# The first 14 steps of two fused layers, issued from one written-out sequence of operations

## The chip, the cores and the metric

The kernel runs on one core of one Trainium2 chip. Its engines are TensorE (PE in the profile; its weight loads are PEld), VectorE (DVE), ScalarE (ACT), GpSimd (POOL) and SyncE (SP), which here only issues DMAs. Each engine executes its own queue of instructions strictly in the order in which the program put them there, and waits on semaphores for the other engines. The metric is the device time of one execution in microseconds, as the median of several executions.

## The reference

```python
def sm(a, b):                      # softmax over the last axis
    s = scale * (a @ b.transpose(0, 2, 1))
    e = np.exp(s - s.max(-1, keepdims=True))
    return e / (e.sum(-1, keepdims=True) + 1e-09)
agent_v = sm(agents, k) @ v        # 49 agents over 12480 tokens of 128 features
x = sm(q, agents) @ agent_v        # 12480 x 128

h = x @ w_in                       # layer 1, 128 -> 2048
g = np.where(h >= 1, h, np.where(h <= -1, 0.0, (h + 1) ** 2 / 4))
x = g @ w_out                      # 2048 -> 128
h = x @ w_in2                      # layer 2, 128 -> 2048
g = s * np.maximum(h, 0) ** 2 + b
out = g @ w_out2
```

## The kernel before

The 12480 tokens are cut into 25 blocks: the first of 256, 23 of 512, the last of 448. A prologue (some 66 us) loads keys, values and weights, splits each weight into a high and a low part, and folds the agents' values into the first layer's weights (`awh`, `awl`). Then comes a loop of *steps*. A step `n` of a layer is two of the 16 slices of 128 hidden features of one block, so a block has 8 steps; steps 0 to 7 are the block of 256 tokens (tiles of 128x512 elements), the later ones blocks of 512 (128x1024).

The operations of a step, with the lines of the profile. Layer 1: `H(1, n)` (L567, PE, the products into a PSUM tile `h`), `relu` (L583, ACT, reads `h`, writes `x`), `square` (L589, ACT, `x` in place), `cap` (L593, DVE, reads `h` and `x`, writes `x`), `hi` (the high part `gh`, on ACT at L602 or on DVE at L604), `lo` (the low part `gl`, DVE, L609), `O(1, n)` (L649, PE, six matmuls into `y` from `gh` and `gl`). Layer 2 has `H(2, m)`, `relu` (L585), `square`, `hi`, `lo` and `O(2, m)` into `o`, without a cap. When a block's eight `O(1)` are done, `evac(1, ...)` copies `y` to `yh` (ACT, L668) and `yl` (DVE, L671), the input of layer 2. The caption of a tile tells the layer only with its buffer numbers; `x_14` is step 14.

For each block there is a softmax over the agents as well: `q_scores` (PE, L153, tile `qs`), a copy (ACT, L160, `qe`), maximum, difference (DVE), exponential (ACT, L174), sum, 1e-9, reciprocal, product (DVE), and the high and low halves of `ptok` (DVE, L182, L183); then `q_transpose` (PE, L196, `tp`) and a copy to `pt` (ACT, L201), which `H(1)` reads.

What sets the order: the program runs under a manual schedule, so each engine's queue has the order in which Python calls the operations. In the loop, step `n` puts on PE, in this order, `H(1, n)`, the scores of a softmax if one is due, a transpose if due, `O(1, n-2)`, `H(2, m)`, `O(2, m-2)` with `m = n - 11` (string `POR`); and on ACT and DVE the order of `ORD`, or of `ORDR` in the first 11 steps. The DVE and ACT operations of a softmax wait in the list `fillers` and are issued one at a time, one by each `lo` and one by each letter F; `q_transpose` first issues all that are left (L192). `sums_column` (three DVE operations on `csum` and `bcol`) goes through the same list, from step 11 on.

PSUM: all of `h`, `qs` and `tp` share one ring of 3 tiles of two banks; `y` and `o` have one bank each. `x`, `gh` and `gl` have 4 buffers each in SBUF.

`PAT1` tells for steps 0 to 10 of layer 1 whether `hi` runs on ACT (1) or DVE (0), and it is DVE after that.

Of the kernel before, what the change touches and what calls it, by code (L numbers as in the profile page):

```python
# [18 lines left out]
def kernel(  # L19
# [24 lines left out]

    GR, XB, UB, WB, KV = 4, 4, 4, 2, 7
    WARM, CD = 10, 1
    PAT1, PAT2, TL = "01010101010", "11011101", 11

# [16 lines left out]
        "A0 k0 k1 A1 k2 k3 k4 B0 k5 k6 k7 k8 B1 k9 k10 k11 k12 C0 q0 v0 v1 v2 C1 v3 v4 v5 v6 D0 v7 v8 v9 v10 v11 "  # L67
        "v12 D1 q1"
    )
    WORD = "A0 A1 B0 B1 C0 C1 D0 D1".split()  # L70
    POR = "H1 QS QT O1 H2 O2".split()
    NR, ORDR, ORD = 11, (
        "T2 R1 Y y R2 Q G2 C2 S1 M1 c1 G1 L1 L2 Z F"
    ).split(), (
        "R1 T2 S1 Q Y G2 R2 C2 L1 F M1 y L2 F Z G1 c1"
    ).split()
    QS, QT, DX = (7, 6, 3), (6, 5, 1), 1
    MASK_H = 0x7FFFFE00
    WBIAS = -8.0 * 896 * 2 ** 20
    TB = 512  # L80
# [65 lines left out]
    def q_scores(t):  # L146
        if t >= NB:
            return []
        qt = q_t.pop(t)
        sc = ps_h(f"qs{t}")  # L150
        scv = sc[:, 0, 0:4 * NA].rearrange("p (c a) -> p c a", a=NA)
        for i, c0 in enumerate(subs(t)):
            nc.tensor.matmul(out=scv[:, i, :], lhsT=qt[:, c0:c0 + P], rhs=aT, start=True, stop=True)  # L153
        e = small.tile([P, 4, NA], F32, tag="qe", name=f"qe{t}")
        mx = small.tile([P, 4], F32, tag="qm", name=f"qm{t}")
        sm = small.tile([P, 4], F32, tag="qsm", name=f"qsm{t}")
        pt = ptok[t % NPT]
        parts = [(P, 0, len(subs(t)))]
        ops = [
            lambda n=n, a=a, b=b: nc.scalar.activation(out=e[:n, a:b, :], in_=scv[:n, a:b, :], func=ACTF.Copy)  # L160
            for n, a, b in parts
        ]
        qev.extend(ops)
        ops = []
        for n, a, b in parts:
            ev, mv, sv = e[:n, a:b, :], mx[:n, a:b], sm[:n, a:b]
            wide = [n, b - a, NA]
            ph, pl = pt[:n, a:b, 0:NA], pt[:n, a:b, LO:LO + NA]
            ops += [
                lambda ev=ev, mv=mv: nc.vector.tensor_reduce(out=mv, in_=ev, op=ALU.max, axis=AX.X),  # L170
                lambda ev=ev, mv=mv, wide=wide: nc.vector.tensor_tensor(
                    out=ev, in0=ev, in1=mv.unsqueeze(2).to_broadcast(wide), op=ALU.subtract
                ),
                lambda ev=ev: nc.scalar.activation(out=ev, in_=ev, func=ACTF.Exp, scale=scale),  # L174
                lambda: None,
                lambda ev=ev, sv=sv: nc.vector.tensor_reduce(out=sv, in_=ev, op=ALU.add, axis=AX.X),
                lambda sv=sv: nc.vector.tensor_scalar_add(sv, sv, 1e-9),
                lambda sv=sv: nc.vector.reciprocal(out=sv, in_=sv),
                lambda ev=ev, sv=sv, wide=wide: nc.vector.tensor_tensor(
                    out=ev, in0=ev, in1=sv.unsqueeze(2).to_broadcast(wide), op=ALU.mult  # L180
                ),
                lambda ev=ev, ph=ph: nc.vector.tensor_copy(out=ph, in_=ev),  # L182
                lambda ev=ev, ph=ph, pl=pl: nc.vector.tensor_tensor(  # L183
                    out=pl, in0=ev, in1=ph.bitcast(F32), op=ALU.subtract
                ),
            ]
        return ops

    def q_transpose(t):
        if t >= NB:  # L190
            return
        fill(len(fillers))  # L192
        w = blocks[t][1]
        tp = ps_h(f"tp{t}")[:, 0, :]
        for i, c0 in enumerate(subs(t)):
            nc.tensor.matmul(  # L196
                out=tp[:, c0:c0 + P], lhsT=ptok[t % NPT][:, i, :], rhs=ident_r,
                start=True, stop=True,
            )
        pt_t[t] = ptp.tile([P, TB], F32R, tag="pt", name=f"pt{t}")  # L200
        qev.append(lambda: nc.scalar.activation(out=pt_t[t][:, :w], in_=tp[:, :w], func=ACTF.Copy))  # L201
# [333 lines left out]
    def sums_column():  # L535

        c = csum.rearrange("p (k d) -> p k d", d=P)
        return [
            lambda: nc.vector.tensor_tensor(
                out=c, in0=c, in1=ident.unsqueeze(1).to_broadcast([P, TB // P, P]), op=ALU.mult  # L540
            ),
            lambda: nc.vector.tensor_reduce(out=bcol, in_=csum, op=ALU.add, axis=AX.X),
            lambda: nc.vector.tensor_scalar_mul(bcol, bcol, b_sb[:, 0:1]),
        ]
# [9 lines left out]
    def H(layer, n):  # L554
        t, j = divmod(n, JP)
        w = blocks[t][1]
        h = ps_h(f"h{layer}_{n}")
        for i in range(2):
            sl = slice((2 * j + i) * P, (2 * j + i + 1) * P)
            if layer == 1:  # L560
                rhs = pt_t[t][:, :w]
                ops = [(awh, rhs), (awl, rhs)]
            else:
                yh, yl = y_hl[t]
                ops = [(wi2h, yh[:, :w]), (wi2h, yl[:, :w]), (wi2l, yh[:, :w])]
            for m, (a, r) in enumerate(ops):
                nc.tensor.matmul(  # L567
                    out=h[:, i, :w], lhsT=a[:, sl], rhs=r, start=(m == 0), stop=(m == len(ops) - 1)
                )
        hp[layer, n] = h  # L570
# [8 lines left out]
    def relu(layer, n):  # L579
        gx[layer, n] = ring("x", layer, n, F32, XB)  # L580
        x, h = gv(gx, layer, n), gv(hp, layer, n)
        if layer == 1:
            nc.scalar.activation(out=x, in_=h, func=ACTF.Relu, scale=0.5, bias=0.5)  # L583
        else:
            nc.scalar.activation(out=x, in_=h, func=ACTF.Relu)  # L585

    def square(layer, n):
        x = gv(gx, layer, n)
        nc.scalar.activation(out=x, in_=x, func=ACTF.Square)  # L589
# [5 lines left out]
    def hi(layer, n, on_act):  # L595
        kind = GH(layer, n)
        if (kind == "1") != on_act:
            return
        gh[layer, n] = ring("gh", layer, n, F32R, GR)
        x, a = gv(gx, layer, n), gv(gh, layer, n)  # L600
        if on_act:
            nc.scalar.activation(out=a, in_=x, func=ACTF.Copy)  # L602
        else:
            nc.vector.tensor_copy(out=a, in_=x)  # L604
# [12 lines left out]
    def GH(layer, n):  # L617
        if layer == 1:
            return PAT1[n] if n < len(PAT1) else "0"
        return PAT2[n % len(PAT2)] if n < NS - TL else "0"  # L620
# [37 lines left out]
    def evac(layer, part):  # L658
# [14 lines left out]
        else:  # L673
# [5 lines left out]
            nc.sync.dma_start(out=outT[:, t0:t0 + w], in_=osb[:, :w])  # L679
            del done[2]  # L680

    with tc.manual_schedule():
        prologue()
        late = ctx.enter_context(tc.tile_pool(name="late", bufs=1))
        for n in range(NS + D + D2):
            t, j = divmod(n, JP)
            m = n - D
            a1, a2, b2 = n < NS, 0 <= m < NS, 0 <= m - 1 < NS
            b1 = 0 <= n - 1 < NS
            if j == 0:  # L690
                load_q(t + 2)
            for c in POR:
                if c == "H1" and a1: H(1, n)
                if c == "H2" and a2: H(2, m)
                if c == "O1" and 0 <= n - D1 < NS: O(1, n - D1)
                if c == "O2" and 0 <= m - D2 < NS: O(2, m - D2)
                if c == "QS" and n == 0: fillers.extend(q_scores(1))
                if c == "QS" and j == QS[min(t, 2)]: fillers.extend(q_scores(t + 2))
                if c == "QT" and j == QT[min(t, 2)]: q_transpose(t + 1)
            if n == NR:  # L700
                fillers.extend(sums_column())
            if m == NS:
                last_step(False)
            b2 = 0 <= m - 1 < NS - 1
            a2 = 0 <= m < NS - 1
            for c in (ORDR if n < NR else ORD):
                if c == "T2" and b2: square(2, m - 1)
                if c == "Q": q_evac()
                if c == "Y": evac(1, "h")
                if c == "y": evac(1, "l")  # L710
                if c == "Z": evac(2, "")
                if c == "G2" and b2: hi(2, m - 1, True)
                if c == "G1" and a1: hi(1, n, True)
                if c == "R1" and a1: relu(1, n)
                if c == "S1" and a1: square(1, n)
                if c == "R2" and a2: relu(2, m)
                if c == "M1" and a1: cap(n)
                if c == "c1" and a1: hi(1, n, False)
                if c == "C2" and b2: hi(2, m - 1, False)
                if c == "L1" and b1: lo(1, n - 1)  # L720
                if c == "L2" and b2: lo(2, m - 1)
                if c == "F": fill()
            if m == NS - 1:
                last_step(True)
# [35 lines left out]
```

## Time and profile before

| | us |
|---|---|
| median of 3 executions (1128.07 to 1128.37) | 1128.16 |
| the profiled execution | 1129.3 |
| its span, first to last instruction | 1126.6 |
| PE busy | 1093.7 |
| DVE busy | 986.5 |
| ACT busy | 971.8 |

The profile is of one execution. Its times count from the first instruction of the span. Busy times of an engine count overlapping instructions once; a matmul's end is modelled. "Granted clock" is the clock that TensorE was given, as a share of 2.4 GHz: 1.00, or 0.50 for 1.2 GHz. In the span's stretch up to about 66 us stands the prologue; step 0 of layer 1 begins at 66.28 us, step 14 at 114.05 us.

### The profile page before, as it was taken

The page shows a single profiled execution, that of the slowest core. Times are in us where ns is not written, and L with a number is a line of the kernel's source. Part 1 is how long each engine was busy: PE and PEld are TensorE (multiplying, and loading weights), DVE is VectorE, ACT ScalarE, POOL GpSimd, SP SyncE. Part 2 cuts the span into 40 slices and gives each one's busy share as a digit, 9 for nine tenths or more (in the row PEclk, how much of TensorE's full clock was granted, in tenths as well). Part 3 has the DMA queues.
Part 4 walks back from the last instruction along what each step waited for, and adds up shares of the span by engine and source line. Part 5 has one row for each costly group of instructions (what it writes and reads, how often), then busy time and mean ns, then how long its engine had stood idle before and what let it go on. Part 6 is the DMA issues. An engine that isn't in the chain of part 4 may idle for free.

```text
span 1126.6 us, 13210 instructions
## 1 busy us (share of the span) xinstructions
PE 1093.7 (97%) x5044; PEld 883.1 (78%) x5044; DVE 986.5 (88%) x1191; ACT 971.8 (86%) x1128; POOL 0.9 (0%) x7
## 2 busy tenths in 40 slices
PE   7877999999999999999999999999999999999998
PEld 3665888888888888888888888888888888888887
DVE  7867998898898898898898898898898898898886
ACT  6966899889889889889889888888888888889886
POOL 0000000000000000000000000000000000000000
PEclk9988999999999999999999999999999999999999
DMA  9910000000000000000000000000000000000000
GB/s 354 394 40 10 1 15 19 1 19 19 1 19 19 1 19 19 1 19 19 1 19 19 1 19 19 1 20 19 1 19 20 1 19 18 1 10 10 1 10 17
DMA packets 16254, 34.81 MB, mean 31 GB/s; under 512 B 1792, under 2 KB 6720, under 8 KB 15680
## 3 DMA queue, kind: packets, MB, share of 16 engines
q1 hardware_dynamic: 16192, 33.98, 8.5%
q8 instruction: 39, 0.64, 0.2%
q14 instruction: 23, 0.19, 0.1%
HBM read 27.58 MB, written 6.39 MB: 30 GB/s over the span
## 4 chain that ended last, share of the span: by engine, by line
PE 91%; DVE 5%; ACT 2%; DMA 1%; issue 0%; SPq 0%; DVEq 0%
PE h L567 39%; PE o L649 24%; PE y L649 24%; PE qs L153 2%; DVE x L593 1%; DMA k<-in_kT 1%; PE tp L196 1%; DVE gl L609 1%; PE av L422 1%; ACT x L589 1%; DVE mxs L379 1%; ACT x L583 1%; PE st L405 0%; DVE wt L264 0%; DVE gh L604 0%
## 5 line engine op out<-in xcount | busy, mean ns | idle before, releaser
L609 DVE TENSOR_TENSOR gl<-x,gh 128x1024 fp32r<-128x1024 f32 (+2 forms) x399 | 476.2, 1194 | 7.9 <-ACT gh L602 0.2
L589 ACT ACTIVATE x<-x 128x1024 f32<-128x1024 f32 (+2 forms) x399 | 392.0, 1033 | 0.6
L593 DVE SCALAR_TENSOR_TENSOR x<-h,x 128x1024 f32<-128x1024 f32 (+2 forms) x200 | 238.9, 1194 | 65.8 <-ACT x L589 62.8
L583 ACT ACTIVATE x<-h 128x1024 f32<-128x1024 f32 (+2 forms) x200 | 201.5, 1007 | 109.7 <-PE h L567 109.5
L585 ACT ACTIVATE x<-h 128x1024 f32<-128x1024 f32 (+2 forms) x199 | 199.2, 1001 | 11.1 <-PE h L567 11.1
L604 DVE CAST gh<-x 128x1024 fp32r<-128x1024 f32 (+2 forms) x252 | 170.6, 677 | 39.8 <-ACT x L589 39.5
L649 PE MATMUL y<-gl,wo1h 128*128 128x512 f32 (+2 forms) x400 | 158.1, 395 | 11.0 <-DVE gl L609 11.0
L649 PE MATMUL y<-gh,wo1h 128*128 128x512 f32 (+2 forms) x400 | 160.3, 401 | 1.4 <-DVE yl L671 0.9
L567 PE MATMUL h<-pt,awh 128*128 128x512 f32 (+2 forms) x400 | 157.0, 393 | 0.4 <-ACT qe L160 0.4
L649 PE MATMUL y<-gh,wo1l 128*128 128x512 f32 (+2 forms) x400 | 156.7, 392 | 0.0
L567 PE MATMUL h<-pt,awl 128*128 128x512 f32 (+2 forms) x400 | 156.5, 392 | 0.0
L567 PE MATMUL h<-yl,wi2h 128*128 128x512 f32 (+2 forms) x400 | 156.1, 390 | 0.0
L567 PE MATMUL h<-yh,wi2h 128*128 128x512 f32 (+2 forms) x400 | 156.1, 390 | 0.0
L567 PE MATMUL h<-yh,wi2l 128*128 128x512 f32 (+2 forms) x400 | 156.0, 390 | 0.0
L649 PE MATMUL o<-gl,wo2h 128*128 128x512 f32 (+2 forms) x400 | 155.9, 390 | 0.0
L649 PE MATMUL o<-gh,wo2l 128*128 128x512 f32 (+2 forms) x400 | 155.8, 389 | 0.0
L649 PE MATMUL o<-gh,wo2h 128*128 128x512 f32 (+2 forms) x400 | 155.7, 389 | 0.0
L602 ACT ACTIVATE gh<-x 128x1024 fp32r<-128x1024 f32 (+1 forms) x147 | 150.6, 1024 | 5.3 <-DVE x L593 5.3
L649 PEld LDWEIGHTS y<-gl,wo1h 128*128 128x128 f32 x400 | 76.2, 190 | 30.0 <-DVE gl L609 13.1
L567 PEld LDWEIGHTS h<-pt,awh 128*128 128x128 f32 x400 | 76.4, 191 | 17.3 <-ACT qe L160 0.5
L649 PEld LDWEIGHTS y<-gh,wo1h 128*128 128x128 f32 x400 | 76.4, 191 | 16.8 <-DVE yl L671 1.3
L567 PEld LDWEIGHTS h<-pt,awl 128*128 128x128 f32 x400 | 76.3, 191 | 16.6
(109 smaller groups left out, 956.8 us busy)
## 6 DMA issues: line engine op xcount, KB each, us to landing
k<-in_kT SPq DMA_DIRECT2D x12, 512.0 KB, 11.4
v<-in_v_main SPq DMA_DIRECT2D x12, 512.0 KB, 9.3
q<-in_qT SPq DMA_DIRECT2D x23, 256.0 KB, 2.7
out_T<-osb SPq DMA_DIRECT2D x23, 256.0 KB, 2.0
wu<-in_w_out SPq DMA_DIRECT2D x4, 1024.0 KB, 10.7
wu<-in_w_in SPq DMA_DIRECT2D x4, 1024.0 KB, 12.2
q<-in_qT SPq DMA_DIRECT2D x1, 224.0 KB, 2.5
out_T<-osb SPq DMA_DIRECT2D x1, 224.0 KB, 1.9
```

The source lines that it names most:

```text
L153: nc.tensor.matmul(out=scv[:, i, :], lhsT=qt[:, c0:c0 + P], rhs=aT, start=True, stop=True)
L196: nc.tensor.matmul(out=tp[:, c0:c0 + P], lhsT=ptok[t % NPT][:, i, :], rhs=ident_r, start=True, stop=True,)
L379: nc.vector.tensor_reduce(out=mxs[r, g:g + 1], in_=ST[r, c], op=ALU.max, axis=AX.X)
L567: nc.tensor.matmul(out=h[:, i, :w], lhsT=a[:, sl], rhs=r, start=(m == 0), stop=(m == len(ops) - 1))
L583: nc.scalar.activation(out=x, in_=h, func=ACTF.Relu, scale=0.5, bias=0.5)
L585: nc.scalar.activation(out=x, in_=h, func=ACTF.Relu)
L589: nc.scalar.activation(out=x, in_=x, func=ACTF.Square)
L593: nc.vector.scalar_tensor_tensor(out=x, in0=h, scalar=1.0, in1=x, op0=ALU.max, op1=ALU.min)
L602: nc.scalar.activation(out=a, in_=x, func=ACTF.Copy)
L604: nc.vector.tensor_copy(out=a, in_=x)
L609: nc.vector.tensor_tensor(out=b, in0=x, in1=a.bitcast(F32), op=ALU.subtract)
L649: nc.tensor.matmul(out=o[:, :w], lhsT=l[:, c, :], rhs=r[:, i, :w], start=(c == 0 and m == 0), stop=(c == KF - 1 and m == 2),)
```

## The change

A string `RAMP` now holds the operations of the first 14 steps one by one, in one sequence, and a function `ramp` calls them in that order; the loop begins at step 14 (`NR`). The operations are the same: 14 `H` and 12 `O` of layer 1, three `H` and one `O` of layer 2, and their elementwise work. So are the softmaxes of blocks 1 and 2 (tokens `q`, `z`, `p`, `P`), which no longer go through `fillers`. `H` stands up to four steps ahead of `O`. `sums_column` goes to `fillers` after the sequence. `PAT1` has 14 digits: the `hi` of layer 1 ran on ACT in steps 1, 3, 5, 7 and 9, and runs there now in steps 0, 3, 4, 6, 10 and 13.

```diff
-    PAT1, PAT2, TL = "01010101010", "11011101", 11
+    PAT1, PAT2, TL = "10011010001001", "11011101", 11
+    RAMP = (
+        "u2 H0 q1 R0 H1 S0 z1.0 M0 R1 z1.1 H2 g0 z1.2 H3 z1.3 L0 S1 z1.4 O0 R2 M1 R3 z1.5 H4 g1 z1.6 S2 L1 S3 z1.7 "
...
+    )
-    NR, ORDR, ORD = 11, (
-        "T2 R1 Y y R2 Q G2 C2 S1 M1 c1 G1 L1 L2 Z F"
-    ).split(), (
+    NR, ORD = 14, (
         "R1 T2 S1 Q Y G2 R2 C2 L1 F M1 y L2 F Z G1 c1"
     ).split()
-    QS, QT, DX = (7, 6, 3), (6, 5, 1), 1
+    QS, QT, DX = (6, 3), 1, 1
+    def ramp():
+        steps = {}
+
+        def first_q(k):
+            ops = q_scores(k)
+            steps[k] = [q_evac, *ops[:3], *ops[4:]]
+
+        does = {
+            "H": lambda n: H(1, n), "R": lambda n: relu(1, n), "S": lambda n: square(1, n), "M": cap,
+            "g": lambda n: hi(1, n, GH(1, n) == "1"), "L": lambda n: lo(1, n), "O": lambda n: O(1, n),
+            "h": lambda n: H(2, n), "r": lambda n: relu(2, n), "s": lambda n: square(2, n),
+            "G": lambda n: hi(2, n, GH(2, n) == "1"), "l": lambda n: lo(2, n), "o": lambda n: O(2, n),
+            "Y": lambda: evac(1, "h"), "y": lambda: evac(1, "l"),
+            "u": load_q, "q": first_q, "p": q_transpose, "P": lambda n: q_evac(), "z": lambda k, i: steps[k][i](),
+        }
+        for token in RAMP.split():
+            does[token[0]](*[int(x) for x in token[1:].split(".") if x])
...
-        for n in range(NS + D + D2):
+        ramp()
+        fillers.extend(sums_column())
+        for n in range(NR, NS + D + D2):
...
-                if c == "QS" and n == 0: fillers.extend(q_scores(1))
-                if c == "QS" and j == QS[min(t, 2)]: fillers.extend(q_scores(t + 2))
-                if c == "QT" and j == QT[min(t, 2)]: q_transpose(t + 1)
-            if n == NR:
-                fillers.extend(sums_column())
+                if c == "QS" and j == QS[t > 1]: fillers.extend(q_scores(t + 2))
+                if c == "QT" and t > 1 and j == QT: q_transpose(t + 1)
```

In the changed kernel every line number is 7 higher (L593 is L600, L609 is L616). The queue of DVE at the start of step 0, before: here `x` is the cap, `gh` the cast, `gl` the low part, `q..` the softmax of block 1.

```order
L593 SCALAR_TENSOR_TENSOR x_0_660<-h_0_647,x_0_660 128x2x256
L604 CAST gh_0_665<-x_0_660 128x2x256
L170 TENSOR_REDUCE qm_658<-qe_657 128x4
L593 SCALAR_TENSOR_TENSOR x_1_673<-h_1_668,x_1_673 128x2x256
L609 TENSOR_TENSOR gl_0_679<-x_0_660,gh_0_665 128x2x256
L171 TENSOR_TENSOR qe_657<-qe_657,qm_658 128x196
L593 SCALAR_TENSOR_TENSOR x_2_695<-h_2_683,x_2_695 128x2x256
L604 CAST gh_2_699<-x_2_695 128x2x256
L609 TENSOR_TENSOR gl_1_701<-x_1_673,gh_1_677 128x2x256
L176 TENSOR_REDUCE qsm_659<-qe_657 128x4
```

The same place on DVE after the change.

```order
L600 SCALAR_TENSOR_TENSOR x_0_660<-h_0_647,x_0_660 128x2x256
L177 TENSOR_REDUCE qm_658<-qe_657 128x4
L178 TENSOR_TENSOR qe_657<-qe_657,qm_658 128x196
L616 TENSOR_TENSOR gl_0_687<-x_0_660,gh_0_678 128x2x256
L183 TENSOR_REDUCE qsm_659<-qe_657 128x4
L600 SCALAR_TENSOR_TENSOR x_1_670<-h_1_662,x_1_670 128x2x256
L184 TENSOR_SCALAR qsm_659<-qsm_659 128x4
L611 CAST gh_1_709<-x_1_670 128x2x256
L185 RECIPROCAL qsm_659<-qsm_659 128x4
L616 TENSOR_TENSOR gl_1_713<-x_1_670,gh_1_709 128x2x256
```

A `gl` now stands ahead of the next step's cap instead of behind it, and the softmax's operations stand between the others from the start, at most two in a row. On PE the queue was `H` 0, scores, `H` 1, `H` 2, `O` 0, `H` 3, `O` 1; it is now `H` 0, scores, `H` 1, `H` 2, `H` 3, `O` 0, `H` 4, `O` 1.

ACT around the first operations of step 14, before: `x_2` and `gh_1` are layer 2, `x_14` layer 1.

```order
L201 ACTIVATE pt_967<-tp_962 128x512
L602 ACTIVATE gh_1_993<-x_1_946 128x2x256
L585 ACTIVATE x_2_995<-h_2_974 128x2x256
L583 ACTIVATE x_14_1036<-h_14_1004 128x1024
L589 ACTIVATE x_2_995<-x_2_995 128x2x256
L589 ACTIVATE x_14_1036<-x_14_1036 128x1024
```

The same place on ACT after the change.

```order
L609 ACTIVATE gh_1_966<-x_1_941 128x2x256
L596 ACTIVATE x_13_962<-x_13_962 128x1024
L592 ACTIVATE x_2_993<-h_2_978 128x2x256
L208 ACTIVATE pt_992<-tp_987 128x512
L609 ACTIVATE gh_13_999<-x_13_962 128x1024
L590 ACTIVATE x_14_1033<-h_14_1001 128x1024
L596 ACTIVATE x_2_993<-x_2_993 128x2x256
L596 ACTIVATE x_14_1033<-x_14_1033 128x1024
```

The high part of step 13 is now a copy on ACT, between the relu of `x_2` and its square. The DVE instruction that waits for that square (the cast of `x_2`) follows the low part of step 12 on DVE.

DVE around the end of the softmax of block 3, whose transpose stands on PE behind `H(1, 17)`, before.

```order
L178 RECIPROCAL qsm_1016<-qsm_1016 128x4
L179 TENSOR_TENSOR qe_1014<-qe_1014,qsm_1016 128x196
L604 CAST gh_15_1096<-x_15_1079 128x1024
L609 TENSOR_TENSOR gl_15_1132<-x_15_1079,gh_15_1096 128x1024
L182 CAST ptok_89<-qe_1014 128x4x49
L183 TENSOR_TENSOR ptok_89<-qe_1014,ptok_89 128x4x49
L593 SCALAR_TENSOR_TENSOR x_16_1124<-h_16_1100,x_16_1124 128x1024
L609 TENSOR_TENSOR gl_4_1137<-x_4_1085,gh_4_1128 128x2x256
L604 CAST gh_16_1139<-x_16_1124 128x1024
L609 TENSOR_TENSOR gl_16_1183<-x_16_1124,gh_16_1139 128x1024
```

The same place on DVE after the change.

```order
L185 RECIPROCAL qsm_1013<-qsm_1013 128x4
L600 SCALAR_TENSOR_TENSOR x_16_1121<-h_16_1097,x_16_1121 128x1024
L616 TENSOR_TENSOR gl_4_1134<-x_4_1083,gh_4_1125 128x2x256
L186 TENSOR_TENSOR qe_1011<-qe_1011,qsm_1013 128x196
L189 CAST ptok_89<-qe_1011 128x4x49
L611 CAST gh_16_1138<-x_16_1121 128x1024
L190 TENSOR_TENSOR ptok_89<-qe_1011,ptok_89 128x4x49
L616 TENSOR_TENSOR gl_16_1183<-x_16_1121,gh_16_1138 128x1024
```

Since the three operations of `sums_column` now stand ahead of this softmax in `fillers`, its last operations are issued a step later: the low half of `ptok` has moved from ahead of the cap of step 16 to just ahead of the low part of step 16.

## Rows read from the trace of the kernel before

**Rows 1.** The page's head and its chain that ended last, by engine.
```profile
span 1126.6 us, 13210 instructions
PE 91%; DVE 5%; ACT 2%; DMA 1%; issue 0%; SPq 0%; DVEq 0%
```
**Rows 2.** Stretches: length, busy of PE, PEld, DVE, ACT, POOL (instructions), granted clock, DMA.
```profile
66.28:114.05 47.77, 34.21 (x177) 28.91 (x176) 34.39 (x58) 31.22 (x48) 0.00 (x0) 0.86 0.04 11
68.74:130.07 61.33, 47.47 (x253) 40.18 (x252) 48.08 (x80) 43.23 (x65) 0.00 (x0) 0.89 0.03 9
133.08:1119.14 986.06, 986.06 (x4391) 804.10 (x4392) 875.14 (x1012) 873.15 (x972) 0.00 (x0) 1.00 0.04 12
```
**Rows 3.** Waits of PE from 66.3 to the end: total, times, longest.
```profile
PE y L649 <- DVE gl L609: 11.0, 7, 2.9
PE y L649 <- DVE yl L671: 0.9, 1, 0.9
```
**Rows 4.** Waits of DVE from 68.74 to 130.07.
```profile
DVE x L593 <- ACT x L589: 10.5, 8, 2.0
DVE yl L671 <- ACT yh L668: 1.7, 1, 1.7
DVE gh L604 <- ACT x L589: 1.1, 1, 1.1
```
**Rows 5.** Timeline of ACT and DVE at step 0: start, length, [idle before].
```profile
67.07 0.60 ACT L583 ACTIVATE x<-h 128x512 f32<-128x512 f32 x1
68.03 0.62 ACT L589 ACTIVATE x<-x 128x512 f32<-128x512 f32 x1
...
68.74 0.69 DVE L593 SCALAR_TENSOR_TENSOR x<-h,x 128x512 f32<-128x512 f32 x1 [0.94 <-ACT x L589]
```
**Rows 6.** Timeline of DVE at the end of block 3's softmax.
```profile
127.34 0.36 DVE L183 TENSOR_TENSOR ptok<-qe,ptok 128x196 fp32r<-128x196 f32 x1
127.62 1.22 DVE L593 SCALAR_TENSOR_TENSOR x<-h,x 128x1024 f32<-128x1024 f32 x1
128.75 0.68 DVE L609 TENSOR_TENSOR gl<-x,gh 128x512 fp32r<-128x512 f32 x1
129.35 0.68 DVE L604 CAST gh<-x 128x1024 fp32r<-128x1024 f32 x1
130.07 1.23 DVE L609 TENSOR_TENSOR gl<-x,gh 128x1024 fp32r<-128x1024 f32 x1
```
**Rows 7.** Timeline of PE there: block 3's transpose, the end of H 18, O 16.
```profile
127.85 0.63 PE L196 MATMUL tp<-ident_r,ptok 128*128 128x128 f32 x4 [0.73 <-DVE ptok L183]
...
131.83 0.40 PE L567 MATMUL h<-pt,awl 128*128 128x512 f32 x1
133.08 0.50 PE L649 MATMUL y<-gh,wo1h 128*128 128x512 f32 x1 [0.86 <-DVE yl L671]
```
**Rows 8.** ACT instructions by shape, 67.05 to 130: busy, mean ns, idle before.
```profile
L589 ACT ACTIVATE x<-x 128x512 f32<-128x512 f32 x14 | 8.8, 626 | 0.2
L602 ACT ACTIVATE gh<-x 128x1024 fp32r<-128x1024 f32 x1 | 1.1, 1057 | 1.3 <-DVE x L593 1.3
L583 ACT ACTIVATE x<-h 128x1024 f32<-128x1024 f32 x10 | 10.2, 1022 | 2.5 <-PE h L567 2.5
```
**Rows 9.** PE by stretches (length, busy, granted clock); three of its waits.
```profile
72.00:78.75 6.75, 5.30 (x25) 0.50 0.00 0
92.50:95.85 3.35, 3.23 (x10) 0.50 0.00 0
102.60:106.15 3.55, 3.41 (x11) 0.52 0.00 0
...
71.60 0.38 PE L649 MATMUL y<-gl,wo1h 128*128 128x256 f32 x1 [1.15 <-DVE gl L609]
...
92.62 0.58 PE L649 MATMUL y<-gl,wo1h 128*128 128x256 f32 x1 [2.95 <-DVE gl L609]
102.74 0.80 PE L649 MATMUL y<-gl,wo1h 128*128 128x512 f32 x1 [2.48 <-DVE gl L609]
```

More of the change, by code (lines that the diff above doesn't have):

```diff
@@ L705 @@
             a2 = 0 <= m < NS - 1
-            for c in (ORDR if n < NR else ORD):
+            for c in ORD:
                 if c == "T2" and b2: square(2, m - 1)
```

4 rows, old and new, of the table RAMP are left out of this document.

## The prediction

> **What bounds the kernel now.** I read the page's chain first: PE holds 91% of it, DVE 5%, ACT 2% [rows 1]. Then the table of stretches, to see where that is not so. From 133.08 to 1119.14 PE is busy for all of 986.06 us at granted clock 1.00; no reordering of the start reaches that stretch, except by beginning it earlier. From 66.28 (H of step 0) to 114.05 (H of step 14), however, 47.77 us hold 34.21 of PE, 34.39 of DVE and 31.22 of ACT, at clock 0.86 [rows 2]. No engine fills the stretch, so it is made of waits: PE waits 11.0 us in seven pieces for low parts `gl` [rows 3], while DVE waits 10.5 us for squares on ACT, 1.7 for `yh` and 1.1 for a cast's input [rows 4]. The engines pass each step round in a ring of single-step lead. So I read the stretch by the fullest engine, DVE, from cap 0 (68.74) to the place where the two queues have done the same set again, the low part of step 16 (130.07): 61.33 us, 48.08 busy, 13.25 idle [rows 2]. What the change can give is that idle time; what it gives to the end is decided where PE last waits.
>
> **DVE's side.** The change adds no operation. It moves the copy of step 13 from DVE to ACT: DVE saves about 0.65 us (0.68 long at 129.35, next start 0.72 later) [rows 6]. In the old queue the scores' copy stood between relu 0 and square 0 (67.07 and 68.03); now the square comes first, so cap 0 starts some 0.3 us earlier than 68.74 [rows 5]. An operation that follows a wait leaves its predecessor's tail bare: a cap lasts 1.22 but the next starts 1.13 after it [rows 6]; ten waits less [rows 4] are 0.9 us.
>
> What idle time stays? I went through the new queues by hand with durations of the rows (relu and square 0.6 for 256 tokens, 1.0 for 512; cap and low part 0.60 and 1.13 start to start; a handover 0.05 to 0.1), each operation starting when its engine and its inputs are there. Cap 1 finds DVE free at 70.7 and its square just done; cap 4 is free at 75.5, square at 74.0; cap 6 at 78.9 and 78.9; cap 8 at 82.5 and 82.5; cap 10 at 89.2 and 88.0; cap 12 at 95.7 and 94.4. So DVE runs nearly without a break, with no reserve at caps 1, 6 and 8: 0.3 us lost. H four steps ahead is what buys this: each H waits only for a cap to free one of the three `h` tiles, and H 4 (free at 71.5) and H 5 (73.5) then still lie ahead of the relus that read them. One real hole appears. Behind cap 13, ACT does the copy of step 13 (1.06), relu 14 (1.02) and only then square 2 of layer 2 (0.63), whose cast DVE wants next; with overlaps 2.6 us, against 1.13 of low part 12 on DVE [rows 6, 8]: 1.5 us. Left: 1.8 us.
>
> DVE reaches the low part of step 16 earlier by 13.25 + 0.65 + 0.3 + 0.9 - 1.8 = 13.3 us, at 116.8.
>
> **PE's side.** This does not all arrive. PE's last waits before were for block 3's transpose (0.73, start 127.85) and for `yl` ahead of O 16 (133.08) [rows 7]. From the transpose to the end of H 18 (131.83 + 0.23) is 4.21 us of PE work, so a transpose at 128.87 would have given the same end. With `sums_column` ahead of it in the list, the low half of `ptok` is now issued behind cap 16, a low part and a cast: not 2.4 us ahead of low part 16 (127.62 to 130.07) but just ahead of it [rows 6]. So the transpose starts at 116.8 + 0.08 + 0.15 (127.70 to 127.85 in the old run) = 117.0. PE's gain: 128.87 - 117.0 = 11.9 us. Behind it PE has 4.2 us of work before O 16, DVE about 3 before `yl`, so that wait should vanish and none should follow.
>
> **The clock.** PE reaches that transpose early. Ahead of it stands O 3 of layer 2, which waits for a low part with 5.8 us of DVE work between it and the end of `ptok`; PE needs 1.6 of them for the rest of O 3 and H 17. So PE stands for some 4.2 us, longer than any wait of the old trace. There, after waits of 2.95 and 2.48 us, PE resumed at 92.62 and 102.74 with the clock at 1.2 instead of 2.4 GHz, for 3.35 and 3.55 us in which it was busy almost throughout (3.23 and 3.41) [rows 9]. Half of 3.4 is 1.7 us, and here nothing hides it, since PE has no later wait. Bounds: 0, if the clock holds, and 3.4, if the low stretch is as long as the one of 6.75 us at 72.00. I take 1.7, the nearer two rows. PE's lower clock costs it nothing else.
>
> **Small things.** SP's loads: block 2's stands where it did, block 3's is some steps ahead of its scores; neither is waited for. `sums_column` is needed at the first output, six steps on, and is already in the DVE sum. For a handover that is later than in my walk (three caps have no reserve) I allow 0.6, from bounds of 0 and 3 (0.2 for each of some 15 handovers).
>
> **Sum.** 11.9 - 1.7 - 0.6 = 9.6 us. The profiled execution took 1129.3 with a span of 1126.6 [rows 1]; it becomes 1119.7 with 1117.0. The median shown is 1.14 lower, so the median becomes 1118.6.
>
> **Rivals.** *The clock holds at the transpose, or PE's stand there is short*: 11.9 less 0 to 0.6, 1116.5. For it: of PE's seven waits for `gl` [rows 3] not every one was followed by a fall; against: the two longest were [rows 9]. 17%.
>
> *The ramp is only half closed.* DVE has no reserve at caps 1, 6 and 8. If the clock falls inside the ramp as it did at 72.00, shortly after a wait of only 1.15 us [rows 9], PE loses up to half of 6.75 = 3.4 us, and O 3, O 4 and H 8 come late for cap 8; about 3 of these 3.4 reach DVE, since up to H 7 PE has slack. 9.6 - 3 = 6.6: 1121.6. For it: the new ramp still makes PE wait 0.4 to 1.4 us before most low parts. Against: 28.2 us of PE work at full clock (worked out below) now lie in some 32 us, not in 47.8. The Trainium skill speaks for this rival: TensorE: Matmul & The Clock Gate, section "A second HAM failure mode: psum-queue depth-cycling", says that short idle pieces of TensorE between groups of matmuls, if frequent, can make the clock swing between its levels. The trace bears it out in part: the fall at 72.00 is one of this kind, the other two followed long waits, and none came after 106.15. 25%, with other causes of a late square.
>
> *The order does not do what it says*: three `h` tiles are shared with scores and transposes, so H could wait for a cap as before and most of DVE's 13.25 us stay. Half of them staying gives 3 us: 1125. Against it: the frees that I found above. 7%, a part of it (4%) within 0.2% of the old time, which is what a measurement here can tell from no change.
>
> *Slower, by one mechanism*: the clock falls early in the ramp and stays low through it. PE's 34.21 us contain 5.30 + 3.23 + 3.41 at the low level [rows 2, 9], so 28.2 at full clock and 56.5 at half, against the 47.77 of now: 8.7 us later at step 14, 1137. It decides from about 40 us at the low level on (half of 40 is lost, and 28.2 + 20 passes 47.77). Against it: all three low stretches ended within 6.75 us, with PE busy. 3%.
>
> **How the numbers follow.** Forecast 48% (1117 to 1120.2 by its own bounds), clock holds 17%, half-closed ramp 25%, little or nothing 7%, slower 3%. Faster by over 0.2% (2.3 us): 48 + 17 + 25 + 3 = 93%; same 4%; slower 3%. For eight in ten I go from 1115.8 (clock holds, no allowance, and 0.5 for the rounding of my walk) to 1122.8 (half-closed ramp with another us of late squares).
>
> **What would show it.** H 14 starts 15 to 16 us earlier (near 98 to 99), cap 14 some 13 to 14. DVE's idle time from cap 0 to the low part of step 16 falls from 13.25 to about 2, the largest piece being the wait of the cast of `x_2` for ACT. PE's longest wait after the change is the one for block 3's `ptok`, 3 to 4.5 us, followed by some 3.4 us at granted clock 0.5; no wait after that. Wrong would be: a DVE idle time above 5 us in the ramp, a second low stretch of the clock between 70 and 95, no wait at the transpose, or a new wait of PE in the long stretch behind it.

## The result, and the profile after

The changed kernel takes 1118.97 us (median of 4 executions, 1118.04 to 1119.31), the kernel before 1128.26 beside it (4 executions, 1128.07 to 1129.91): ratio 0.9913, 95% interval 0.9896 to 0.993. The forecast was 1118.6, the range 1115.8 to 1122.8. The sum agrees to 0.4 us; its terms, as shown below, agree less well and nearly cancel.

The head of the page and the chain that ended last, against [rows 1]:

```profile
span 1117.4 us, 13210 instructions
...
PE 92%; DVE 5%; DMA 2%; ACT 1%; issue 1%; SPq 0%; DVEq 0%; ACTq 0%
```

The table of stretches, against [rows 2]: length, busy time of PE, PEld, DVE, ACT, POOL with numbers of instructions, granted clock, DMA share, GB/s. The stretches are the end of the prologue; `H` of step 0 to `H` of step 14; cap 0 to the low part of step 16; a piece at low clock; and the rest.

```profile
64.30:67.60 3.30, 3.30 (x9) 2.50 (x9) 2.80 (x4) 2.01 (x4) 0.00 (x0) 0.50 0.00 0
68.03:99.98 31.95, 29.91 (x178) 24.42 (x176) 30.68 (x55) 29.72 (x48) 0.00 (x0) 1.00 0.06 17
70.17:117.93 47.76, 41.83 (x240) 33.98 (x238) 45.80 (x78) 42.02 (x65) 0.00 (x0) 1.00 0.04 12
118.90:122.85 3.95, 3.95 (x17) 3.44 (x16) 2.30 (x4) 1.97 (x4) 0.00 (x0) 0.57 0.00 0
122.85:1117.40 994.55, 990.96 (x4415) 807.87 (x4414) 878.74 (x1018) 875.89 (x977) 0.00 (x0) 1.00 0.04 12
```

Step 0 to step 14 takes 31.95 us instead of 47.77, and PE, DVE and ACT are now each busy for 29.7 to 30.7 of them. DVE's idle time between cap 0 and the low part of step 16 is 47.76 - 45.80 = 1.96 us, where it was 13.25.

The waits of DVE between those two operations, against [rows 4], and then those of PE from 66 us on, against [rows 3]: total, times, longest.

```profile
DVE gh L611 <- ACT x L596: 1.4, 1, 1.4
DVE x L600 <- ACT x L596: 0.6, 1, 0.6
```

```profile
PE tp L203 <- DVE ptok L190: 4.0, 1, 4.0
PE y L656 <- DVE gl L616: 1.3, 4, 0.5
```

The eight waits of a cap for a square (10.5 us) have shrunk to one of 0.6, which ends where cap 0 starts. The seven waits of PE for a low part (11.0 us) are four of 1.3 us in all. What is new is one wait of 4.0 us for block 3's `ptok`, as forecast.

PE's timeline, against [rows 7]: the first scores of the sequence, `H` 14, the transpose of block 3, two matmuls behind it, and the scores of block 4 (start, length, [idle before]).

```profile
68.63 1.09 PE L160 MATMUL qs<-a,q 128*128 128x49 f32 x8
...
99.98 0.50 PE L574 MATMUL h<-pt,awh 128*128 128x512 f32 x1 [0.29 <-ACT x L592]
...
118.17 0.63 PE L203 MATMUL tp<-ident_r,ptok 128*128 128x128 f32 x4 [4.01 <-DVE ptok L190]
...
118.93 0.63 PE L656 MATMUL y<-gh,wo1l 128*128 128x512 f32 x1
...
122.34 0.28 PE L656 MATMUL o<-gh,wo2h 128*128 128x256 f32 x1
...
127.65 0.77 PE L160 MATMUL qs<-a,q 128*128 128x49 f32 x6
```

A matmul of this shape takes 0.39 to 0.40 us at full clock; here it takes 0.63, and the slow stretch reaches from 118.93 to about 122.2. PE has no wait between 118.17 and the end.

The first line shows something else: the first scores start at 68.63, where the kernel before had them at 66.75. TensorE's instructions ahead of them are the same; but in the first stretch of the table (64.30 to 67.60) the granted clock was 0.50, and in the profile of the kernel before it was 1.00 there. So I measure all kernels by their own marks: from the first scores in the sequence (block 1's) to the scores of block 4, the *stage*, and from there to the end. The marks are of the one profiled execution of each kernel; each ratio is to the kernel before as it ran beside that kernel (medians of 1128.26 to 1129.19 us).

| kernel | median us | ratio to before, 95% | first scores | stage | rest of span |
|---|---|---|---|---|---|
| before | 1128.26 | 1 | 66.75 | 70.13 | 989.72 |
| changed | 1118.97 | 0.9913 (0.9896 to 0.993) | 68.63 | 59.02 | 989.75 |
| changed, repeated | 1118.54 | 0.9911 (0.9898 to 0.9925) | 67.62 | 59.23 | 989.75 |
| e1 sums later | 1116.85 | 0.9894 (0.988 to 0.9908) | 67.63 | 58.10 | 989.77 |
| e2 PE busy at transpose | 1116.88 | 0.9896 (0.9883 to 0.991) | 66.91 | 57.94 | 989.75 |
| e3 before, PE busy | 1127.67 | 0.9995 (0.9986 to 1.0004) | 66.56 | 69.09 | 989.75 |
| e4 before, new copies | 1130.74 | 1.0011 (1.0002 to 1.002) | 66.52 | 71.36 | 989.72 |
| e5 `H` later | 1124.91 | 0.9958 (0.9944 to 0.9971) | 67.72 | 65.62 | 989.76 |
| e6 softmaxes in the list | 1123.18 | 0.9963 (0.9949 to 0.9976) | 66.70 | 64.74 | 989.76 |
| e7 transpose later | 1116.63 | 0.9888 (0.9874 to 0.9902) | 66.54 | 57.81 | 989.75 |
| e8 e7 and a square earlier | 1113.97 | 0.9866 (0.9849 to 0.9883) | 66.58 | 54.91 | 989.75 |

The last column is the same in all of them within 0.05 us: nothing after block 4's scores pays or loses. The stages of the changed kernel and of its repeat differ by 0.2 us. The change gains 11.1 us in the stage and its profiled execution gives 1.9 back in the prologue; 9.2 is the difference of the spans.

### The profile page after: what moved, and what is told of

The parts are those of the page before. It is cut to its first block, busy times and chain, and to the rows that moved or that the text cites. A ratio compares the mean times of both kernels' runs of the same rounds, so it can differ in the third digit from the quotient of the medians.

```text
span 1117.4 us, 13210 instructions
## 1 busy us (share of the span) xinstructions
PE 1092.8 (98%) x5044; PEld 882.1 (79%) x5044; DVE 984.4 (88%) x1190; ACT 971.2 (87%) x1129; POOL 0.9 (0%) x7
## 4 chain that ended last, share of the span: by engine, by line
PE 92%; DVE 5%; DMA 2%; ACT 1%; issue 1%; SPq 0%; DVEq 0%; ACTq 0%
PE h L574 40%; PE o L656 24%; PE y L656 24%; PE qs L160 2%; DMA wu<-in_w_out 2%; DVE x L600 1%; PE av L429 1%; PE tp L203 1%; DVE gl L616 1%; PE st L412 0%; DVE gh L611 0%; DVE wt L271 0%; PE aw L467 0%; DVE wt L266 0%; ACT wt L261 0%
## 5 line engine op out<-in xcount | busy, mean ns | idle before, releaser
L616 DVE TENSOR_TENSOR gl<-x,gh 128x1024 fp32r<-128x1024 f32 (+2 forms) x399 | 475.8, 1193 | 7.8 <-ACT gh L609 0.2
L600 DVE SCALAR_TENSOR_TENSOR x<-h,x 128x1024 f32<-128x1024 f32 (+2 forms) x200 | 238.4, 1193 | 55.7 <-ACT x L596 52.7
L609 ACT ACTIVATE gh<-x 128x1024 fp32r<-128x1024 f32 (+1 forms) x148 | 151.6, 1025 | 1.3 <-DVE x L600 1.3
L574 PEld LDWEIGHTS h<-yh,wi2h 128*128 128x128 f32 x400 | 75.4, 189 | 17.5 <-DVE x L600 0.4
L656 PEld LDWEIGHTS o<-gl,wo2h 128*128 128x128 f32 x400 | 75.1, 188 | 17.7 <-DVE gl L643 0.3
## 6 DMA issues: line engine op xcount, KB each, us to landing
wu<-in_w_out SPq DMA_DIRECT2D x4, 1024.0 KB, 10.8
```

The costliest lines, as they stand in the source:

```text
L574: nc.tensor.matmul(out=h[:, i, :w], lhsT=a[:, sl], rhs=r, start=(m == 0), stop=(m == len(ops) - 1))
L600: nc.vector.scalar_tensor_tensor(out=x, in0=h, scalar=1.0, in1=x, op0=ALU.max, op1=ALU.min)
L616: nc.vector.tensor_tensor(out=b, in0=x, in1=a.bitcast(F32), op=ALU.subtract)
L656: nc.tensor.matmul(out=o[:, :w], lhsT=l[:, c, :], rhs=r[:, i, :w], start=(c == 0 and m == 0), stop=(c == KF - 1 and m == 2),)
```

## The experiments

**Repeat.** The changed kernel as it is, for the experiments beside it.

> The changed kernel once more, as the yardstick of the others. 1118 to 1119.5 us, 8 to 10.5 us below the kernel before; PE's wait for block 3's ptok about 4 us, then some 3.5 to 4 us at granted clock 0.5.

Measured: 1118.54 us, stage 59.23, the same wait of 4.0 us. The first scores stand at 67.62, so their place also differs between two executions of one kernel.

**e1: `sums_column` later.** Its three operations go into the list only at step 17.

```diff
-        fillers.extend(sums_column())
...
+            if n == 17:
+                fillers.extend(sums_column())
```

> sums_column goes to the list three steps later, behind block 3's transpose, so that the low half of ptok stands ahead of cap 16 again. Theory (the transpose holds PE up): the wait falls from 4.0 us to about 1, the clock stays at 1.00, and the end comes 1.4 (the wait) + 1.9 (the clock) = 3.3 us earlier than the changed kernel's: 1115.6, between 1114.8 and 1116.8. Rival (what PE loses there is given back later, since DVE is behind anyway): 1118.5 to 1119.5, with a new wait of PE for a low part or yl of 2 us or more.

Measured: 1116.85 us. PE's timeline at the transpose and at `O` 16:

```profile
113.80 0.63 PE L203 MATMUL tp<-ident_r,ptok 128*128 128x128 f32 x4 [1.32 <-DVE ptok L190]
...
120.35 0.50 PE L656 MATMUL y<-gh,wo1h 128*128 128x512 f32 x1 [2.18 <-DVE yl L678]
```

Counted from the first scores, the transpose starts 3.5 us earlier than in the repeat (46.17 against 49.69), but the stage is only 1.1 us shorter. PE now reaches `O` 16 before `yl`, on a DVE queue in which the two long operations of `sums_column` (1.3 us) stand ahead of it, and the clock fell behind this wait instead (0.50 from 121.7 to 124.6). The rival had named this second wait, which the wait for `ptok` had covered; the time lies between the two, 0.05 us above the theory's range. The four executions took 1115.04 to 1117.51 us, and the profiled one is the slowest of them; the two fastest have the highest mean granted clocks (0.997 and 0.998, the others 0.992 and 0.993), so the fall of the clock need not be in all of them.

**e2: PE kept busy at the transpose.** 17 matmuls whose product nobody reads go into `tp` ahead of block 3's transposes.

```diff
+        for i in range(17 if t == 3 else 0):
+            nc.tensor.matmul(out=tp, lhsT=wi2h[:, 0:P], rhs=awh[:, 0:TB], start=True, stop=True)
```

> 17 matmuls of 128x512 without use (their tile is overwritten) ahead of block 3's transposes fill PE's wait; nothing else differs from the changed kernel. At 0.22 us each they take 3.7 of the 4.0 us. Theory (the fall of the clock behind the wait is paid in full): clock 1.00 behind the transpose and 1.7 to 2.0 us earlier than the changed kernel: 1117.1. Rival (the low clock costs nothing there, because DVE sets the pace): no difference, 1118.5 to 1119.5.

Measured: 1116.88 us, 1.7 below the repeat, stage 1.3 shorter. PE's timeline: the last ten of the 17 unread matmuls, the transposes and the first products behind them.

```profile
114.75 2.43 PE L203 MATMUL tp<-awh,wi2h 128*128 128x512 f32 x10
117.02 0.56 PE L205 MATMUL tp<-ident_r,ptok 128*128 128x128 f32 x4
117.41 0.45 PE L658 MATMUL y<-gh,wo1h 128*128 128x512 f32 x1
117.70 0.39 PE L658 MATMUL y<-gh,wo1l 128*128 128x512 f32 x1
```

The transposes start no earlier (50.11 us after the first scores, 49.54 and 49.69 in the two profiles of the changed kernel), but the matmuls behind them take 0.39 us and not 0.63, and block 4's scores follow the transposes after 7.83 us (117.02 to 124.85) instead of 9.54 in the repeat. So the clock's price was real and what the prediction took, 1.7.

**e3: the kernel before with PE kept busy.** If the low clock of the old stretch (0.86) had cost what it seems to, this alone would win.

```diff
+    IDLE = (5, 6, 6, 6, 5, 5, 5, 10, 7, 9)
...
+                if c == "O1" and 2 <= n <= 11:
+                    idle = ps_o("idle")
+                    for i in range(IDLE[n - 2]):
+                        nc.tensor.matmul(out=idle, lhsT=awh[:, 0:P], rhs=awh[:, 0:TB], start=True, stop=True)
```

> The kernel before, with 5 to 10 matmuls without use into the o bank ahead of each O of layer 1 in steps 2 to 11, so that PE does not idle and the clock should stay at 1.00 in the first steps; order unchanged. Theory (the old order's ring of waits is the cost, the low clock only a part of it): 2 to 5 us faster than before, 1123.5 to 1126.5, with DVE's idle time between cap 0 and the low part of step 16 still above 8 us. Rival (the three low stretches of the clock are the cost, and the change gains by removing them): 8 to 10 us faster, 1118 to 1120. Second rival (the low clock was hidden by DVE and ACT): no change, 1128.

Measured: 1127.67 us, no difference that these runs can tell. Its stretch from `H` 0 to 1.2 us past `H` 14, with the clock; the start of `H` 14; and DVE's waits for squares, against [rows 2] and [rows 4]:

```profile
66.10:114.00 47.90, 43.63 (x248) 36.81 (x247) 34.44 (x58) 31.68 (x49) 0.00 (x0) 1.00 0.04 12
112.81 0.39 PE L568 MATMUL h<-pt,awh 128*128 128x512 f32 x1
```

```profile
DVE x L594 <- ACT x L590: 10.7, 8, 2.2
```

The clock is 1.00 throughout, and again eight caps wait for squares. `H` 14 starts 46.25 us after the first scores, 47.30 in the kernel before, and the stage is 1.0 us shorter: the wait of a cast of layer 2 for a square, 1.1 us in [rows 4], is gone. So the theory's 2 to 5 us did not come; but "hidden entirely", the second rival, is not shown either, because the unread matmuls hold PE up themselves. An example on DVE and PE at `O` 6:

```profile
87.09 0.68 DVE L610 TENSOR_TENSOR gl<-x,gh 128x512 fp32r<-128x512 f32 x1
...
88.24 1.32 PE L699 MATMUL idle<-awh 128*128 128x512 f32 x5
...
89.63 0.28 PE L650 MATMUL y<-gl,wo1h 128*128 128x256 f32 x1
```

The low part is there at 87.77, `O` 6 reads it at 89.63, behind the unread matmuls and without a wait. Cap 6 is still 0.6 us ahead of the kernel before (17.01 against 17.62 us after the first scores), cap 8 is 0.8 behind it (24.04 against 23.26). What the 13.65 us at half clock [rows 9] cost the old stretch therefore stays open: 1.0 us is what was won net of this, and 6.0, half of PE's 11.94 us of work in them, is the most that PE can have lost there, an estimate from [rows 9] and less than the first rival's 8.

The first rival, that the low clock was the cost, is answered better by the old trace. In it PE by stretch (length, busy, granted clock) and two caps of DVE:

```profile
78.75:89.50 10.75, 8.19 (x58) 1.00 0.09 26
89.50:92.50 3.00, 0.17 (x2) 1.00 0.00 0
...
84.37 0.69 DVE L593 SCALAR_TENSOR_TENSOR x<-h,x 128x512 f32<-128x512 f32 x1 [1.97 <-ACT x L589]
90.01 1.23 DVE L593 SCALAR_TENSOR_TENSOR x<-h,x 128x1024 f32<-128x1024 f32 x1 [1.90 <-ACT x L589]
```

Caps 6 and 8 waited 1.97 and 1.90 us in a stretch with the clock at 1.00, so these waits arise without slow matmuls.

**e4: the new copies alone.** The kernel before with the new `PAT1`.

```diff
-    PAT1, PAT2, TL = "01010101010", "11011101", 11
+    PAT1, PAT2, TL = "10011010001001", "11011101", 11
```

> The kernel before with the new PAT1 alone (which engine does the high parts of the first 14 steps). Theory (the order closes the waits, not the shares of the engines): no difference to before beyond 1.5 us, 1127 to 1129.5; DVE still idles 11 us or more between cap 0 and the low part of step 16. Rival (the better balance of ACT and DVE is much of the gain): 3 us or more faster, below 1125.5.

Measured: 1130.74 us, ratio 1.0011 (1.0002 to 1.002). This is 1.2 us above the expected range. The copies moved to ACT gain nothing in the old sequence; from cap 0 to the low part of step 16 DVE is busy for 47.50 of 62.54 us and idles for 15.0. What the new copies are worth inside the new sequence was not tried.

**e5: each `H` later.** The sequence as changed, but on PE each `H` of steps 3 to 13 stands behind `O` of three steps before; ACT's and DVE's queues are the changed kernel's.

```diff
-        "u2 H0 q1 R0 H1 S0 z1.0 M0 R1 z1.1 H2 g0 z1.2 H3 z1.3 L0 S1 z1.4 O0 R2 M1 R3 z1.5 H4 g1 z1.6 S2 L1 S3 z1.7 "
+        "u2 H0 q1 R0 H1 S0 z1.0 M0 R1 z1.1 H2 g0 z1.2 z1.3 L0 S1 z1.4 O0 H3 R2 M1 R3 z1.5 g1 z1.6 S2 L1 S3 z1.7 "
...
```

> The changed kernel with every H of steps 3 to 13 on PE again behind the O three steps before it, as in the kernel before; ACT's and DVE's queues are unchanged. Theory (the order of ACT and DVE gives most, the lead of H a part: by the chain low part, O, H, relu, square, caps 5 to 8 come 0.6 to 1.3 us later each): 1.5 to 4 us slower than the changed kernel, 1120 to 1122.5. Rival (the lead of H is what closes the waits): 5 us or more lost, above 1123.5. Second rival (the lead is worth nothing): 1118 to 1119.5.

Measured: 1124.91 us; the stage is 6.4 us longer than in the repeat. Two of ACT's waits (relus 6 and 7) and then one of DVE's, at caps 6 and 7:

```profile
81.63 0.60 ACT L590 ACTIVATE x<-h 128x512 f32<-128x512 f32 x1 [1.58 <-PE h L574]
83.76 0.60 ACT L590 ACTIVATE x<-h 128x512 f32<-128x512 f32 x1 [1.54 <-PE h L574]
```

```profile
84.91 1.29 DVE L600 SCALAR_TENSOR_TENSOR x<-h,x 128x512 f32<-128x512 f32 x2 [3.40 <-ACT x L596]
```

An `H` that is late by a low part makes the relu late, that the square (square 6 stands behind relu 7 on ACT), that the cap, and that the next low part: the old ring. PE also waited 1.47 us at 79.09 and its clock was 0.51 from 80.30 to 83.80, with 3.50 of 3.50 us busy; up to half of these 3.50 us, an estimate, is the clock's part in cap 6's wait. The rival was right: without the lead more than half of the gain is lost.

**e6: the softmaxes back in the list.** The sequence as changed, without the tokens `z` but the first of each softmax, which puts the other operations into the list.

```diff
...
-            steps[k] = [q_evac, *ops[:3], *ops[4:]]
+            steps[k] = [lambda: (q_evac(), fillers.extend([*ops[:3], *ops[4:]]))]
```

> The sequence as in the changed kernel, but the VectorE and ScalarE steps of both first softmaxes are taken out of it and issued one per low-part product from a list, as the kernel before does, the rest in one piece ahead of the transposes of block 1. Theory (what pays is the shorter lead of the products and the queues that fit it; the softmax steps' exact places are worth little): 1 to 3 us above the changed kernel, so 1119.5 to 1121.5 us, with one or two VectorE or TensorE waits of 1 to 2 us around the transposes of block 1. First rival (the places of the softmax steps are a main part of the gain): 1122.5 us or more, with waits of over 4 us in all there. Second rival (they count for nothing): within 0.5 us of the changed kernel's 1118.6.

Measured: 1123.18 us, stage 64.74. The softmax's operations on DVE ahead of block 1's transpose and the cap behind them that waits; then PE at the transpose.

```profile
75.69 0.35 DVE L182 TENSOR_REDUCE qsm<-qe 128x4 f32<-128x196 f32 x1
...
77.18 0.36 DVE L189 TENSOR_TENSOR ptok<-qe,ptok 128x196 fp32r<-128x196 f32 x1
...
86.06 1.23 DVE L599 SCALAR_TENSOR_TENSOR x<-h,x 128x1024 f32<-128x1024 f32 x1 [1.93 <-ACT x L595]
```

```profile
77.69 0.63 PE L202 MATMUL tp<-ident_r,ptok 128*128 128x128 f32 x4 [2.33 <-DVE ptok L189]
...
79.51 0.41 PE L573 MATMUL h<-pt,awl 128*128 128x256 f32 x1
```

Six operations that are short, but together, end 10.8 us after the first scores instead of 7.4 in the changed kernel (76.00). PE stands 2.33 us at the head of its queue, the products behind the transpose run at 0.41 instead of 0.28 us, and step 8's cap waits 1.93 us for a square. The first rival was right: the stage is 5.5 us longer than in the repeat, and the waits of 2.33 and 1.93 us come to its 4 us and more. Block 2's transpose then makes PE wait for another 1.69 us. e5 and e6 together would come to 11.9 of the 11.1 us gained, so the two parts are not shares of a sum: either one alone brings waits of the ring back.

**e7: block 3's transpose one step later**, behind `H` 18.

```diff
-                if c == "QT" and t > 1 and j == QT: q_transpose(t + 1)
+                if c == "QT" and t > 1 and j == QT + (t == 2): q_transpose(t + 1)
```

> The changed kernel with block 3's transpose one step later on PE, behind H 18. The run with sums_column late gave only 1.7 us: there DVE stood 2.0 us for the copy of block 3's scores, and PE's wait moved to yl. Here DVE's queue stays as it is, but for the low half of ptok behind low part 16. Theory: PE waits about 1 us for ptok and about 1 for yl in place of 4.0, the clock stays at 1.00, and O 16 comes about 3 us earlier: 1115.5, between 1114.7 and 1116.5. Rival (whatever is taken from this wait comes back at yl): 1117 or more, with a wait of 2 us or more for yl.

Measured: 1116.63 us, stage 1.4 shorter than in the repeat. The wait of 4.0 us falls apart into two. The first ends with a relu of ACT, just behind `ptok`; the second is the one that e1 found (the wait of DVE that the expectation ascribes to block 3's softmax is block 4's):

```profile
117.47 0.63 PE L203 MATMUL tp<-ident_r,ptok 128*128 128x128 f32 x4 [1.15 <-ACT x L590]
119.11 0.79 PE L656 MATMUL y<-gh,wo1h 128*128 128x512 f32 x1 [1.01 <-DVE yl L678]
```

The clock fell here too: it was 0.57 from 118.9 to 122.8. The theory had it at 1.00; the time lies 0.13 us above its range and below the rival's.

**e8: e7, and the square of step 2 of layer 2 ahead of the copy of step 13** in ACT's queue, against the hole at the cast of `x_2`.

```diff
...
-        "R13 z2.9 M12 G1 o0 S13 l1 h2 g12 p2 r2 M13 P2 L12 g13"
...
+        "L11 s1 l0 O11 R13 z2.9 M12 G1 o0 S13 l1 h2 g12 p2 r2 s2 M13 P2 L12 g13"
...
-                if c == "T2" and b2: square(2, m - 1)
+                if c == "T2" and b2 and m > 3: square(2, m - 1)
```

> The same, and square 2 of layer 2 moved ahead of the copy of step 13 and of relu 14 on ACT, so that DVE's wait of 1.4 us for it should go. Theory (DVE sets the pace up to O 16, so each us of its idle time is a us of the end): another 1.0 to 1.5 us, 1114.2, between 1113.3 and 1115.2. Rival (DVE's wait only moves to the next square): no difference to the kernel with the late transpose.

Measured: 1113.97 us, the best of all, ratio 0.9866 (0.9849 to 0.9883). Its whole stage, and PE's two longest waits in it:

```profile
66.58:121.49 54.91, 50.87 (x301) 42.35 (x300) 53.36 (x88) 48.97 (x76) 0.00 (x0) 1.00 0.04 10
```

```profile
116.01 0.63 PE L203 MATMUL tp<-ident_r,ptok 128*128 128x128 f32 x4 [0.87 <-DVE ptok L190]
...
117.65 0.50 PE L656 MATMUL y<-gh,wo1h 128*128 128x512 f32 x1 [1.00 <-DVE yl L678]
```

The hole on DVE is gone and the clock holds 1.00; the stage is 2.9 us shorter than e7's. `O` 16 starts 51.07 us after the first scores instead of 52.57, which is the hole; from there to block 4's scores it takes 3.84 us instead of 5.24, which is the clock's price: this execution did not pay it, although the waits at the transpose are like e7's. The four executions took 1113.11, 1113.25, 1114.68 and 1114.82 us and the profiled one is the fastest, so the clock may have fallen in the two slower ones; no trace shows them. DVE is now busy for 53.36 of 54.91 us: this stage is at the limit of its fullest engine.

## Why the prediction was right

The steps, on the scale from the first scores, so that the prologue stays out of it (the old run had them at 66.75):

- **DVE's idle time.** Forecast 1.8 us left, measured 1.96. The hole at the cast of `x_2`, forecast 1.5, measured 1.42, is the first row here; the second is cap 14, the last two are the end of block 3's softmax and the low part of step 16 (DVE's timeline, against [rows 6]):

```profile
103.56 0.43 DVE L611 CAST gh<-x 128x512 fp32r<-128x512 f32 x1 [1.42 <-ACT x L596]
...
106.37 1.22 DVE L600 SCALAR_TENSOR_TENSOR x<-h,x 128x1024 f32<-128x1024 f32 x1
...
117.66 0.36 DVE L190 TENSOR_TENSOR ptok<-qe,ptok 128x196 fp32r<-128x196 f32 x1
117.93 1.22 DVE L616 TENSOR_TENSOR gl<-x,gh 128x1024 fp32r<-128x1024 f32 x1
```

  `H` 14 starts 15.95 us earlier (47.30 to 31.35), cap 14 (106.37) 14.4 earlier; 15 to 16 and 13 to 14 were forecast, so cap 14 came a little earlier still. The low half of `ptok` stands just ahead of low part 16, as the order said.
- **The term that was too small.** DVE's low part 16 comes 14.0 us earlier (63.32 to 49.30), not 13.3. Its busy time over the same operations fell by 2.28 (48.08 to 45.80); the copy of step 13 is 0.7 of it, so tails (the ends of operations that the next one now overlaps) are 1.6, where I took 0.9 for ten waits. The transpose follows: 12.6 us instead of 11.9.
- **The allowance** of 0.6 for late handovers was not needed.
- **The clock.** PE's stand: forecast 4.2, measured 4.01. From the transpose to block 4's scores the changed kernel takes 9.48 us; the old run's two pieces without a wait are 4.21 (127.85 to 132.06, the end of `H` 18) and 3.80 (133.08 to 136.88), 8.01 at full clock. The low clock cost 1.47, forecast 1.7; against e2, where the clock does not fall and the same takes 7.83, it is 1.65.
- So the stage gained 12.6 - 1.5 = 11.1 us where 9.6 were forecast, and the profiled execution lost 1.9 in the prologue, a term that the sum did not have. That the total fits to 0.4 us is in part luck: 1.5 us too little gain in the stage and 1.9 lost ahead of it nearly cancel.

Of the rivals, the half-closed stretch did not occur here: the clock was 1.00 from 68.03 to 117.93, four waits of up to 0.5 us notwithstanding, so the swing that the Trainium skill describes (TensorE: Matmul & The Clock Gate, "A second HAM failure mode: psum-queue depth-cycling") was not seen. But e5 and e6 show how little reserve there was. Each of them, with a late `H` or a late softmax, lost 5.5 to 6.4 us, with one more stretch at half clock and waits for squares back, where I took 3 us for the rival; they changed the order as well, so they do not measure the rival's own price. Two of the caps that I found without reserve (1, 6, 8) are where the longest waits of a cap came: cap 6 in e5, cap 8 in e6.

The reasoning behind "slower" (a low clock through the sequence) was not put to the test: in no run of the new sequence did the clock stay low for more than some 4 us ahead of step 14.

The 1.9 us of the prologue go with the clock granted there. The stretch from 40 to 50 us in the changed kernel, in e1 and in e3, whose first scores stand at 68.63, 67.63 and 66.56 us:

```profile
40.00:50.00 10.00, 9.86 (x115) 8.61 (x113) 6.09 (x12) 8.21 (x17) 0.00 (x0) 0.81 1.03 411
40.00:50.00 10.00, 9.71 (x118) 8.45 (x116) 6.80 (x13) 8.90 (x19) 0.00 (x0) 0.86 1.02 409
40.00:50.00 10.00, 9.41 (x133) 8.02 (x132) 8.17 (x15) 10.00 (x22) 0.00 (x0) 1.00 1.02 408
```

e5 has 0.86 there as well (67.72), the kernel before and e2 0.93 and 0.91 (66.75 and 66.91), e4, e6, e7 and e8 0.95 to 0.98 (66.52 to 66.70). Only the changed kernel and its repeat have a second low stretch, of some 3 us from about 64 us on; the repeat, with 1.00 from 40 to 50, has its first scores at 67.62 for it.

Left open: why the clock falls at these places in one execution and not in another, with the same instructions; and how much of the 9.3 us difference of the medians rests on it.

## What to carry to other kernels

In a ring of handovers between in-order queues, read the gain from the idle time of the fullest engine, and walk the new queues by hand for the places where an engine reaches an operation before its input: the idle time left and the hole came out within 0.2 us here, the gain 0.7 short, for the tails. A low granted clock is paid where no later wait hides it: behind the last wait it cost 1.5 to 1.7 us. Work that is put in to keep an engine busy must not stand ahead of work that others wait for (e3). A long wait that stays covers the next one: shortening 4.0 us gave back 1.1 and 1.4 us of the stage (e1, e7), since PE then waited at `O` 16 and the clock fell behind that wait; closing the hole that made DVE late gave another 1.5 (e8).

## What the runs showed of the hardware

The prologue's end moves with the clock. The first scores started between 66.52 and 68.63 us in eleven profiles with the same instructions of TensorE ahead of them, later where the clock granted from 40 to 50 us was lower (1.00 to 0.81), but for the repeat, which was at half clock from about 64 us. In the latest of them TensorE was also at half clock from 64.30 to 67.60, busy for all of these 3.30 us, behind a wait of 0.88 us at 64.04. And a wait of the same size is not always answered in the same way: behind 1.15 and 1.01 us in e7 the clock fell, behind 0.87 and 1.00 in e8 it did not, nor behind the first wait of 1.32 in e1 (1.00 from 113.8 to 120.3).
